# Accumulators regrouped by 256 rows in a six-layer cross network: PSUM layout, matmul width, head and tail order

## The chip, the cores and the metric

The kernel runs on one NeuronCore of a Trainium2 chip. The metric is the device time of one launch in microseconds (us). Engine names as in the profile: PE is TensorE's matmuls and PEld its weight loads, DVE is VectorE, ACT is ScalarE, POOL is GpSimd, SP is the engine that here only issues transfers.

## What is computed

Six layers of a cross network over 4096 rows of 416 features, in bf16:

```python
B, F, D, L = 4096, 26, 16, 6      # Din = 416
def reference(x0, ws, bs):
    x = x0
    for l in range(ws.shape[0]):
        x = x0 * (x @ ws[l] + bs[l]) + x
    return x
```

Since every x is x0 times something, the kernel keeps the running sum of all products, P = sum of x_l @ W_l, in PSUM, adds the summed bias c_l to it, and forms x = x0 * (P + c_l), where c_l holds the biases up to layer l and one. So the accumulators of a slab live in PSUM through all six layers.

## The kernel before

**Tiling.** Work is transposed: features lie on the partitions, rows on the free axis. The 4096 rows form four slabs s of SB = 1024; a slab has two halves of H = 512 rows and four groups g of G = 256. The 416 features are three chunks c (or m for outputs, k for inputs) of 128, and a tail of 32. The tail of a slab is packed: the 32 features of group g stand on the partitions 32g to 32g+31, so that `x0t_sb`, `xt_sb` and `t32_sb` are 128x256.

**PSUM.** Eight banks of 512 fp32 columns: bank `3*half + m` holds chunk m of one half, bank 6 (TAIL) the packed tail, bank 7 (SPARE) the transposes of input tails, biases and warm-up fills.

**One layer on TensorE** (program order, n = 6s + l):

1. *half A*, `main(0, wait_a)` (helper `tile_mm`, L174): 36 matmuls, 128 inputs to 32 outputs, 512 columns. Each four are the column tiles q = 0 to 3 of one chunk. `wait_a(k)` waits on s_xa for chunk k of the layer before.
2. *rows* (L272): twelve matmuls of 32 inputs (the tail features of group g) to 128 outputs, 256 columns, as row tiles. Two groups of one half share a bank; so they come in batches of 4, 2, 4 and 2, and batches 3 and 4 wait for s_row. Ahead of them are the waits on s_xt (the tail of x) and s_xb (half b). The last one increments s_ti.
3. *tail*: twelve column-tile matmuls of 256 columns into TAIL, and four with the corner weights `wc_sb`; s_to.
4. *half B*, `main(1, None)`: 36 matmuls as in half A, with s_mb after each chunk.

In slab 0 the transposes of the input tails of the next slabs (`tail_transposes`, eight small matmuls) follow half B of layers 1, 2 and 3; the first waits for s_xtl.

**The other engines.** DVE does six SCALAR_TENSOR_TENSOR a layer (L348): three for half a after s_ti, three for half b after s_mb, each reads a bank of 512 and gives x (s_xa, s_xb). ACT adds the tail's bias (`t32_sb`, L387, after s_to), POOL multiplies by x0 (`xt_sb`, L158, s_xt).

**Head.** SP issues in this order: xin (two loads of 256 rows), xtl of slab 0, the transposing load of x0T for rows 512 to 1023, w of layer 1, four loads of wt, w of layers 2 to 5, xtl of the other slabs (L100), x0T of the other slabs. ACT issues w of layer 0, the biases, and wt of layer 0 (four). TensorE meanwhile runs 20 fills, transposes xin (L198), makes the summed biases, and after half A of layer 0 transposes the tails of slab 0. ACT copies them to `x0t_sb` (L377), on which the rows of layer 0 wait (s_te).

**Tail.** For slabs 0 to 2 SP sends the result through DMA transposes. For slab 3 TensorE transposes (L312, L319): first the blocks of half a, then of half b once all of s_xb is there; ACT makes three copies of 128x768 and one of the tail, DVE one, and SP issues four output transfers (L125).

The order on each engine is the program's own[...] and each engine waits on its semaphores where they stand.

Of the kernel before, what the change touches and what calls it, by code (L numbers as in the profile page):

```python
# [6 lines left out]
FP32 = mybir.dt.float32  # L7
ALU = mybir.AluOpType
ACTF = mybir.ActivationFunctionType


def bass_standalone__dcn_v2_cross__recsys_kernel(
# [18 lines left out]
    TAIL, SPARE = 6, 7  # L31
    NFILL = 20

    with ExitStack() as es:
# [14 lines left out]
        t32_sb = sb("t32_sb", [128, 2, G], FP32)  # L49
        xo_sb = sb("xo_sb", [128, NS, NC, SB])  # L50
# [4 lines left out]
        ones_sb = sb("ones_sb", [128, 128])  # L55
# [18 lines left out]
        s_row, s_ti, s_to, s_mb = sem("s_row"), sem("s_ti"), sem("s_to"), sem("s_mb")  # L74
        s_xa, s_xb = sem("s_xa"), sem("s_xb")
        s_ta, s_xt = sem("s_ta"), sem("s_xt")
        s_oT, s_ot, s_otc = sem("s_oT"), sem("s_ot"), sem("s_otc")
        s_pT, s_out = sem("s_pT"), sem("s_out")
# [7 lines left out]

        @block.sync
        def _(sp):
            for h in range(2):
                sp.dma_start(xin_sb[:, 2 * h:2 * h + 2, :], x0_v[:, 2 * h:2 * h + 2, :]).then_inc(s_xin[h], 16)  # L90
            sp.dma_start(xtl_sb[:, 4:JS, :], x0_v[:, 4:JS, DF:D]).then_inc(s_xtl0, 16)
            sp.dma_start_transpose(x0T_sb[:, :, H:SB], x0[H:SB, 0:DF]).then_inc(s_x0T[0], 16)
# [27 lines left out]
            for i in range(4):  # L120
                j = (NS - 1) * JS + 2 * i
                if i == 0:
                    sp.wait_ge(s_oet, 1)
                sp.wait_ge(s_oe[i], 1)
                sp.dma_start(out_v[:, j:j + 2, :], o_sb[:, j:j + 2, :]).then_inc(s_out, 16)  # L125
# [3 lines left out]
        def _(pool):  # L129
            pool.memset(ones_sb[:, :], 1.0).then_inc(s_ones, 1)  # L130
            pool.memset(bsa_sb[0:1, :], 1.0).then_inc(s_set, 1)
            pool.wait_ge(s_ones, 1)
            pool.affine_select(
                out=ident[:, :], in_=ones_sb[:, :], pattern=[[-1, 128]],
                compare_op=ALU.is_equal, fill=0.0, base=0, channel_multiplier=1,
            ).then_inc(s_set, 1)
            pool.affine_select(
# [14 lines left out]
            for s in range(NS):  # L152
                pool.wait_ge(s_te, s + 1)
                for l in range(L):
                    n = s * L + l + 1
                    pool.wait_ge(s_ta, n)
# [15 lines left out]
        def _(pe):  # L172
            def tile_mm(dst, lhsT, rhs, q, start, stop):
                return pe.matmul(  # L174
                    dst, lhsT=lhsT, rhs=rhs, start=start, stop=stop,
# [3 lines left out]
            def tail_transposes(s):  # L179
                for r in range(2):  # L180
                    for g in range(4):
                        j = 2 * g + r
                        src = xin_sb[:, j, DF:D] if s == 0 and j < 4 else xtl_sb[:, s * JS + j, :]
                        ins = tile_mm(
                            ps[32 * g:32 * g + 32, SPARE, r * 128:(r + 1) * 128],
                            src, ident[:, :], g, True, True,
                        )
# [3 lines left out]
            for i in range(NFILL):  # L191
# [243 lines left out]
```

## Time and profile before

| | us |
|---|---|
| median of 13 runs | 141.57 |
| range of the runs | 140.57 to 142.50 |
| the profiled execution, its own time | 140.92 |
| its span, first to last instruction | 138.44 |
| PE busy | 130.8 (94%) |
| PEld busy | 68.3 (49%) |
| DVE busy | 98.7 (71%) |
| ACT, POOL busy | 17.8, 21.2 |
| one layer in the steady part | 5.13 |

The span leaves out what lies around the first and last instruction, here 2.5 us. Matmuls overlap, and their ends are modelled, so TensorE's work is read from the starts: the distance between the starts of two groups is what a group costs. A line such as L174 is that of a helper and gathers matmuls of several kinds.

### The profile page before, as it was taken

What the parts mean: (1) busy time and instruction counts of PE and PEld (TensorE: products, weight loads), DVE (VectorE), ACT (ScalarE), POOL (GpSimd) and SP (SyncE); (2) the same over time, 40 slices, a digit from 0 to 9 for tenths busy, and PEclk for the clock granted to TensorE, in tenths of its full rate; (3) what the DMA queues carried; (4) which work ended last, traced back from release to release, by engine and by line L of the source; (5) the groups of instructions that cost most, each with busy time, mean ns of one, the idle gap of its engine ahead of it and who ended that gap; (6) DMA issues with size and microseconds to landing.
All of it is one profiled execution on the core that took longest, in us unless ns stands there. A gap on an engine that the chain in (4) does not pass through costs nothing.

```text
span 138.4 us, 5386 instructions
## 1 busy us (share of the span) xinstructions
PE 130.8 (94%) x2506; PEld 68.3 (49%) x2506; DVE 98.7 (71%) x149; ACT 17.8 (13%) x36; POOL 21.2 (15%) x44
## 2 busy tenths in 40 slices
PE   6789999999999999999999999999999999999950
PEld 5435447645545445545545445545445545454440
DVE  0308778687688688679679679669669669669660
ACT  0611112111101101101101101101101101101170
POOL 5024111011011021011001111101101201101100
PEclk9999999999999999999999999999999999999999
DMA  4999799920009907000009651000009860000007
GB/s 105 283 252 335 88 231 219 171 60 0 5 0 92 166 1 250 0 0 5 5 0 119 132 195 56 5 0 5 5 0 193 58 231 20 5 0 7 0 2 245
DMA packets 32946, 12.26 MB, mean 89 GB/s; under 512 B 25239, under 2 KB 32925, under 8 KB 32925
## 3 DMA queue, kind: packets, MB, share of 16 engines
q1 hardware_dynamic: 32320, 11.50, 40.7%
q10 hardware_dynamic: 604, 0.43, 1.0%
q8 instruction: 19, 0.31, 0.9%
q14 instruction: 3, 0.02, 0.0%
HBM read 3.22 MB, written 3.41 MB: 48 GB/s over the span
## 4 chain that ended last, share of the span: by engine, by line
PE 90%; DVE 3%; DMA 3%; ACT 1%; SPq 0%; issue 0%
PE ps L174 77%; PE ps L272 12%; DVE xo_sb L348 3%; DMA xin_sb<-in_x_dram 3%; PE ps L312 1%; PE ps L198 1%; ACT o_sb L403 1%; SPq L90 0%; ACT x0t_sb L377 0%
## 5 line engine op out<-in xcount | busy, mean ns | idle before, releaser
L348 DVE SCALAR_TENSOR_TENSOR xT_sb<-ps,cb_sb,x0T_sb 128x512 bf16<-128x512 f32 x120 | 80.9, 743 | 25.6 <-PE ps L272 25.6
L174 PE MATMUL ps<-xT_sb,w_sb 128*32 128x512 bf16 (+1 forms) x1680 | 91.3, 364 | 0.0
L174 PEld LDWEIGHTS ps<-xT_sb,w_sb 128*32 128x32 bf16 x1680 | 44.0, 97 | 36.5 <-issue 0.5
L158 POOL TENSOR_TENSOR xt_sb<-t_sb,x0t_sb 128x256 bf16<-128x256 f32 x20 | 13.5, 674 | 84.6 <-ACT t_sb L387 84.6
L387 ACT ACTIVATE t_sb<-ps,cb_sb 128x256 f32<-128x256 f32 x24 | 11.4, 474 | 103.0 <-PE ps L174 103.0
L174 PE MATMUL ps<-x0T_sb,w_sb 128*32 128x512 bf16 (+1 forms) x336 | 19.7, 378 | 0.0
L348 DVE SCALAR_TENSOR_TENSOR xo_sb<-ps,cb_sb,x0T_sb 128x512 bf16<-128x512 f32 x24 | 16.2, 743 | 4.3 <-PE ps L272 4.3
L272 PE MATMUL ps<-xt_sb,wt_sb 32*128 32x256 bf16 x240 | 15.2, 275 | 0.0
L174 PEld LDWEIGHTS ps<-x0T_sb,w_sb 128*32 128x32 bf16 x336 | 8.8, 99 | 8.0 <-issue 1.0
L272 PEld LDWEIGHTS ps<-xt_sb,wt_sb 32*128 32x128 bf16 x240 | 6.0, 91 | 13.4 <-issue 8.5
L174 PE MATMUL ps<-xt_sb,wc_sb 128*32 128x256 bf16 x80 | 5.7, 273 | 0.0
L158 POOL TENSOR_TENSOR xot_sb<-t_sb,x0t_sb 128x256 bf16<-128x256 f32 x4 | 2.7, 675 | 17.8 <-ACT t_sb L387 17.8
L330 DVE COPY x0T_sb<-ps 128x256 bf16<-128x256 bf16 x4 | 1.2, 292 | 5.2 <-PE ps L198 4.9
L272 PE MATMUL ps<-x0t_sb,wt_sb 32*128 32x256 bf16 x48 | 3.0, 274 | 0.6 <-ACT x0t_sb L377 0.6
L192 PE MATMUL ps<-ones_sb 128*128 128x128 bf16 x20 | 2.3, 313 | 1.1 <-POOL ones_sb L130 1.1
L148 POOL COPY wc_sb<-wt_sb 32x32 bf16<-32x32 bf16 (+1 forms) x8 | 2.1, 258 | 5.4 <-DMA wt_sb<-in_ws_dram 4.9
L272 PEld LDWEIGHTS ps<-x0t_sb,wt_sb 32*128 32x128 bf16 x48 | 1.2, 91 | 3.0 <-issue 2.0
L198 PE MATMUL ps<-ident,xin_sb 128*128 128x128 bf16 x12 | 1.6, 307 | 1.0 <-DMA xin_sb<-in_x_dram 1.0
L403 ACT ACTIVATE o_sb<-ps 128x768 bf16<-128x768 bf16 x3 | 2.3, 809 | 2.2 <-PE ps L312 2.2
L192 PEld LDWEIGHTS ps<-ones_sb 128*128 128x128 bf16 x20 | 2.1, 147 | 1.1 <-POOL ones_sb L130 1.1
L377 ACT ACTIVATE x0t_sb<-ps 128x256 bf16<-128x256 f32 x4 | 1.5, 384 | 7.9 <-PE ps L174 7.9
L312 PE MATMUL ps<-ident,xo_sb 128*128 128x128 bf16 x24 | 1.7, 220 | 0.8 <-DVE xo_sb L348 0.8
(28 smaller groups left out, 16.4 us busy)
## 6 DMA issues: line engine op xcount, KB each, us to landing
out_dram<-o_sb SPq DMA_DIRECT2D x3, 832.0 KB, 4.1
w_sb<-in_ws_dram SPq DMA_DIRECT2D x5, 312.0 KB, 5.1
out_dram<-o_sb SPq DMA_DIRECT2D x4, 208.0 KB, 2.4
wt_sb<-in_ws_dram SPq DMA_DIRECT2D x4, 130.0 KB, 3.9
xin_sb<-in_x_dram SPq DMA_DIRECT2D x2, 208.0 KB, 3.5
w_sb<-in_ws_dram ACTq DMA_DIRECT2D x1, 312.0 KB, 3.7
xtl_sb<-in_x_dram SPq DMA_DIRECT2D x1, 192.0 KB, 7.2
o_sb<-xo_sb SPq DMA_TRANSPOSE x9, 4.4
```

The lines of the kernel that those rows point to most:

```text
L148: pool.tensor_copy(out=wc_sb[p, a:b, p], in_=wt_sb[p, a:b, DF:D]).then_inc(s_wc, 1)
L158: pool.tensor_tensor(out=dst, in0=t32_sb[:, n % 2, :], in1=x0t_sb[:, s, :], op=ALU.mult).then_inc(s_xt, 1)
L174: return pe.matmul(dst, lhsT=lhsT, rhs=rhs, start=start, stop=stop, skip_group_check=True, tile_position=(0, 32 * q),)
L192: pe.matmul(ps[:, SPARE, 0:128], lhsT=ones_sb[:, :], rhs=ones_sb[:, :], start=True, stop=True)
L198: ins = pe.transpose(out=psT[:, NC * (1 - h) + c, (j % 2) * 128:(j % 2 + 1) * 128], in_=xin_sb[:, j, c * 128:(c + 1) * 128], identity=iden ...
L272: ins = pe.matmul(ps[:, NC * (g // 2) + m, (g % 2) * G:(g % 2) * G + G], lhsT=wt_sb[p, l, m * 128:(m + 1) * 128], rhs=srct[p, :], start=l ...
L312: ins = pe.transpose(out=psT[:, banks[i], jj * DF + c * 128:jj * DF + (c + 1) * 128], in_=xo_sb[:, s, c, j * 128:(j + 1) * 128], identity= ...
L330: dve.tensor_copy(out=x0T_sb[:, c, h * 256:(h + 1) * 256], in_=psT[:, NC * (1 - h) + c, 0:256]).then_inc(s_inD, 1)
L348: dve.scalar_tensor_tensor(out=dst, in0=ps[:, NC * half + c, :], scalar=cb_sb[:, c, l:l + 1], in1=x0T_sb[:, c, o:o + H], op0=ALU.add, op1= ...
L377: act.activation(out=x0t_sb[:, s, :], in_=ps[:, SPARE, 0:G], func=ACTF.Copy).then_inc(s_te, 1)
L387: act.activation(out=t32_sb[:, n % 2, :], in_=ps[:, TAIL, 0:G], func=ACTF.Identity, bias=cb_sb[:, NC, l:l + 1],).then_inc(s_ta, 1)
L403: act.activation(out=o_sb[:, j0 + 2 * i:j0 + 2 * i + 2, 0:DF], in_=psT[:, (SPARE, 0, 3, 4)[i], 0:2 * DF].rearrange("p (j d) -> p j d", d=D ...
```

## The change

**PSUM layout.** `acc(m, g)` gives bank and first column: chunks 0 and 1 of group g share bank g, chunk 2 of group g has the first half of bank 4 + g. So group g, and with it row tile g, only ever writes the banks g and 4 + g. TAIL and SPARE move to the second halves of the banks 7 and 6. DVE reads a half of a chunk as two pieces of 256 out of two banks (`acc_half`, `split`).

**Matmul width.** Halves A and B are now done chunk by chunk (`chunk`), for each k with two groups of 256 columns in place of one of 512: 72 matmuls and weight loads a half in place of 36.

**Rows.** Three rounds of four with no s_row.

**Waits.** s_mb is raised twice a layer, after chunks 1 and 2, since chunks 0 and 1 share banks. Before chunk 2 of half B TensorE waits for s_ta (the bias activation has read TAIL). s_xa is awaited for two chunks at once.

**Input tails.** `tail_transposes` of slab s + 1 stand in layer 1 of slab s, between the tail and half B; the first of them still waits for s_xtl. Those of slab 0 go ahead of half A of layer 0.

**Head.** SP issues xin (first half), w of layer 0, xtl of slab 0, two of the four loads of wt of layer 0, then the transposing load; ACT issues xin (second half), the biases and the other two of wt. The fills are 13 of 256 columns, and three more between the two halves of xin's transposes.

**Tail.** In the last layer ACT adds the bias to chunk 2 of half a (into `a32_sb`) and POOL multiplies (s_a32, s_xaP), so DVE leaves it out. The last transposes are split: chunks 0 and 1 of half b before chunk 2. The last output transfer is issued by ACT.

```diff
+        def acc(m, g):
+            return (g, m * G) if m < 2 else (4 + g, 0)
+        def acc_half(m, half):
+            b, c = acc(m, 2 * half)
+            return ps[:, b:b + 2, c:c + G]
+        IN_BANKS = ((2, 3, 6), (4, 5, 2))
+        TAIL = ps[:, 7, G:2 * G]
+        SPARE = ps[:, 6, G:2 * G]
...
         def _(sp):
-            for h in range(2):
-                sp.dma_start(xin_sb[:, 2 * h:2 * h + 2, :], x0_v[:, 2 * h:2 * h + 2, :]).then_inc(s_xin[h], 16)
+            sp.dma_start(xin_sb[:, 0:2, :], x0_v[:, 0:2, :]).then_inc(s_xin[0], 16)
+            sp.dma_start(w_sb[:, 0, :, :], wmain(0)).then_inc(s_w[0], 16)
             sp.dma_start(xtl_sb[:, 4:JS, :], x0_v[:, 4:JS, DF:D]).then_inc(s_xtl0, 16)
+            for g in range(2):
+                sp.dma_start(wt_sb[32 * g:32 * g + 32, 0, :], ws[0, DF:D, :]).then_inc(s_wt[0], 16)
             sp.dma_start_transpose(x0T_sb[:, :, H:SB], x0[H:SB, 0:DF]).then_inc(s_x0T[0], 16)
...
+                    if n == NL:
+                        pool.wait_ge(s_a32, 1)
+                        pool.tensor_tensor(
+                            out=xo_sb[:, s, 2, 0:H], in0=a32_sb[:, :], in1=x0T_sb[:, 2, s * SB:s * SB + H], op=ALU.mult
+                        ).then_inc(s_xaP, 1)
...
             pe.wait_ge(s_ones, 1)
-            for i in range(NFILL):
-                pe.matmul(ps[:, SPARE, 0:128], lhsT=ones_sb[:, :], rhs=ones_sb[:, :], start=True, stop=True)
+            fill(13)
...
+            pe.wait_ge(s_xtl0, 16)
+            pe.wait_ge(s_inD, 2)
+            tail_transposes(0, 6, True)
...
-                    def main(half, waits):
...
+                    def chunk(m, half, before=None):
+                        for k in range(NC):
+                            if before:
+                                before(m, k)
...
+                            if COLUMN_TILES:
+                                for g in range(2 * half, 2 * half + 2):
+                                    b, c = acc(m, g)
+                                    for q in range(4):
+                                        f0 = m * 128 + 32 * q
+                                        ins = tile_mm(
+                                            ps[32 * q:32 * q + 32, b, c:c + G], w_sb[:, l, k, f0:f0 + 32],
+                                            src[:, k, off + g * G:off + (g + 1) * G], q,
+                                            l == 0 and k == 0 and m != 1 and half == 0,
+                                        )
+                        return ins
...
-                    for i, jobs in enumerate((
-                        ((0, 0), (1, 1), (2, 0), (3, 1)), ((0, 2), (2, 2)),
-                        ((0, 1), (1, 0), (2, 1), (3, 0)), ((1, 2), (3, 2)),
-                    )):
-                        if i >= 2:
-                            pe.wait_ge(s_row, 3 * n + i - 1)
-                        for g, m in jobs:
+                    for i in range(NC):
+                        for g in range(4):
+                            m = (i, (i + 2) % NC)[g // 2]
                             p = slice(32 * g, 32 * g + 32)
+                            b, c = acc(m, g)
                             ins = pe.matmul(
-                                ps[:, NC * (g // 2) + m, (g % 2) * G:(g % 2) * G + G],
+                                ps[:, b, c:c + G],
                                 lhsT=wt_sb[p, l, m * 128:(m + 1) * 128], rhs=srct[p, :],
...
-                        if i < 3:
-                            ins.then_inc(s_row, 1)
                     ins.then_inc(s_ti, 1)
...
-                    main(1, None)
-                    if s == 0 and 1 <= l <= NS - 1:
-                        if l == 1:
+                    if l == 1 and s < NS - 1:
+                        if s == 0:
                             pe.wait_ge(s_xtl, 16)
-                        pe.wait_ge(s_te, l)
-                        tail_transposes(l)
+                        tail_transposes(s + 1, 6, False)
+
+                    def before_b(m, k):
+                        if m == 2 and k == 0:
+                            pe.wait_ge(s_ta, n + 1)
+                            if l == 1 and s < NS - 1:
+                                pe.wait_ge(s_te, s + 2)
+
+                    chunk(0, 1, before_b)
+                    chunk(1, 1, before_b).then_inc(s_mb, 1)
+                    chunk(2, 1, before_b).then_inc(s_mb, 1)
...
                             dve.scalar_tensor_tensor(
-                                out=dst, in0=ps[:, NC * half + c, :], scalar=cb_sb[:, c, l:l + 1],
-                                in1=x0T_sb[:, c, o:o + H], op0=ALU.add, op1=ALU.mult,
+                                out=split(dst), in0=acc_half(c, half), scalar=cb_sb[:, c, l:l + 1],
+                                in1=split(x0T_sb[:, c, o:o + H]), op0=ALU.add, op1=ALU.mult,
                             ).then_inc((s_xa, s_xb)[half], 1)
...
         def _(act):
-            act.dma_start(w_sb[:, 0, :, :], wmain(0)).then_inc(s_w[0], 16)
+            act.dma_start(xin_sb[:, 2:4, :], x0_v[:, 2:4, :]).then_inc(s_xin[1], 16)
             act.dma_start(bsa_sb[1:L + 1, :], bs[:, :]).then_inc(s_bs, 16)
-            for g in range(4):
+            for g in range(2, 4):
                 act.dma_start(wt_sb[32 * g:32 * g + 32, 0, :], ws[0, DF:D, :]).then_inc(s_wt[0], 16)
...
+                    if n == NL:
+                        act.wait_ge(s_ti, n)
+                        act.activation(
+                            out=split(a32_sb[:, :]), in_=acc_half(2, 0), func=ACTF.Identity, bias=cb_sb[:, 2, l:l + 1],
+                        ).then_inc(s_a32, 1)
...
+            act.wait_ge(s_oe[3], 2)
+            act.wait_ge(s_oet, 1)
+            act.dma_start(out_v[:, j0 + 6:j0 + 8, :], o_sb[:, j0 + 6:j0 + 8, :]).then_inc(s_out, 16)
```

## Prediction

> **What bounds the kernel now.** First the page: which engine carries the chain that ended last, and who waits for whom.
>
> ```profile
> span 138.4 us, 5386 instructions
> ...
> PE 90%; DVE 3%; DMA 3%; ACT 1%; SPq 0%; issue 0%
> PE ps L174 77%; PE ps L272 12%; DVE xo_sb L348 3%; DMA xin_sb<-in_x_dram 3%; PE ps L312 1%; PE ps L198 1%; ACT o_sb L403 1%; SPq L90 0%; ACT x0t_sb L377 0%
> ...
> L348 DVE SCALAR_TENSOR_TENSOR xT_sb<-ps,cb_sb,x0T_sb 128x512 bf16<-128x512 f32 x120 | 80.9, 743 | 25.6 <-PE ps L272 25.6
> ```
>
> TensorE holds 90% of the chain; DVE waits for it (25.6 us), not the reverse. Then the timeline of one steady layer (start, us, engine, count), to split TensorE's 5.13 us:
>
> ```profile
> 72.79 0.51 PE L174 MATMUL ps<-x0T_sb,w_sb 128*32 128x256 bf16 x12
> ...
> 73.23 2.12 PE L174 MATMUL ps<-x0T_sb,w_sb 128*32 128x512 bf16 x36
> ...
> 75.18 2.12 PE L174 MATMUL ps<-xT_sb,w_sb 128*32 128x512 bf16 x36
> ...
> 77.22 0.76 PE L272 MATMUL ps<-xt_sb,wt_sb 32*128 32x256 bf16 x12
> ...
> 77.92 0.51 PE L174 MATMUL ps<-xT_sb,w_sb 128*32 128x256 bf16 x12
> ...
> 78.25 0.28 PE L174 MATMUL ps<-xt_sb,wc_sb 128*32 128x256 bf16 x4
> ...
> 78.36 0.39 PE L174 MATMUL ps<-xT_sb,w_sb 128*32 128x512 bf16 x4
> ```
>
> Ends of matmuls overlap, so only starts are read. Four column tiles run side by side. Half B (73.23 to 75.18) is 9 groups of four: 0.216 us each. Half A to the rows (75.18 to 77.22) is the same plus 0.095 for the change to row tiles. The twelve row matmuls of L272 take 0.70 (77.22 to 77.92) where three groups at 0.11 would be 0.33. Narrow windows show why: the 2nd, 3rd and 4th batches start at
>
> ```profile
> 77.34 0.27 PE L272 MATMUL ps<-xt_sb,wt_sb 32*128 32x256 bf16 x2
> 77.59 0.29 PE L272 MATMUL ps<-xt_sb,wt_sb 32*128 32x256 bf16 x4
> 77.71 0.28 PE L272 MATMUL ps<-xt_sb,wt_sb 32*128 32x256 bf16 x2
> ```
>
> so batch 2 costs 0.12 for two matmuls, and the s_row wait 0.24 before batch 3. Last, the head: when the load lands that the change puts in front of layer 1's half B.
>
> ```profile
> L100 SPq DMA_DIRECT2D xtl_sb<-in_x_dram x1: 542/542/542, 9.7 to 9.7; - x1
> ...
> DMA to landing us min/median/max: 7.2/7.2/7.2
> ```
>
> Issued at 9.71, xtl lands at 16.9. Today it is needed at 18.3 (TensorE's transposes after B of layer 1): no wait.
>
> [...] groups at 6.58, 7.00, 7.43, 7.86 (0.43), then 0.216 from about 8.2. [...] the windows from 3 to 15 us show a DMA share of 1.05 to 1.43, saturated. [...]
>
> **Part by part, against the profiled run (span 138.4, its own time 140.92, so 2.5 around the span).**
>
> *Row tiles, removed cost.* Three rounds of four, each row tile in banks of its own, no s_row: 0.11 + 0.11 + 0.20 (the last round to the tail, as 77.71 to 77.92) = 0.43 against 0.70: **-0.27 per layer**.
>
> *256 columns in place of 512, added.* 72 matmuls become 144, with 72 more weight loads. Nearest row: the tail groups of 128x256, whose starts are 110, 109 and 109 ns apart (77.92 to 78.25 is three groups). 36 groups x 109.2 = 3.93 against 18 x 215.8 = 3.885: **+0.047 per layer**. The loads (97 ns each, four beside each other) fit in 109 by 12 ns; that cover is thin.
>
> Net -0.22, a period of 4.91. Of 24 layers, 22 (from B of layer 1 to B of layer 23) count: -4.8.
>
> *Does DVE then bound?* L348 starts at 0.31 after the last row batch; five pitches of 0.66 and 0.743 end at 4.36; the xb wait to the first row matmul takes at least 0.11 (9.855 to 9.96 in layer 0), the rows 0.22: 4.7 against 4.91. Reading two banks with a split pattern is not in the trace; from zero to 10 ns each (ACT's four-dimensional L397 takes 392 against 383): 4.76, still hidden. The new s_mb rule lets DVE's b0 start only after chunk 1, since chunks 0 and 1 share banks: chunk 1 is visible 2.15 after the last row batch, DVE is free at 2.30. Hidden by 0.15. s_ta ahead of chunk 2: ACT's 0.47 ends about 0.6 us before it is needed.
>
> *Head.* xin's second half and half of wt move to ACT, w0 and the rest to SP ahead of the x0T transpose, so that five issues (0.5 each) precede it in place of three: w1 and all behind it, xtl too, are issued about 1.0 later (10.7). DMA is saturated, so much of that is backlog; but while SP spends 2.7 us issuing the transpose (3.3 to 6.0) little else is queued, and I estimate that xtl lands 0.3 to 1.0 later, **17.5** taken (16.9 to 18.2 kept). TensorE's own head gains: 16 fills of 256 replace 20 of 128, the first tail transposes move ahead of A, and ACT's x0t copy (0.38, from 9.43) and the idle around it leave the path: rows of layer 0 at about 8.4 to 9.3 in place of 9.96. POOL's larger memset (0.2 before) and its new order end before xin lands at 3.9; its wc copies get wt no later than now (7.3). w1, 1.0 later, lands near 10; A of layer 1 asks for it near 12. Layer 1 then reaches its tail's end at about 14.8 to 15.3 in place of 16.3.
>
> *Where that gain goes.* The transposes of slab 1 now stand before B of layer 1, behind s_xtl. TensorE, arriving near 15, stops until 17.5: **2.2 to 2.7 us idle**, with everything on its queue behind it. After the landing, 0.1 for the wait and 0.11 for eight transposes: B starts at 17.7 against 16.36 before: **+1.35**. The head's gain is worth nothing; it only lengthens the wait. A second effect: [...] after, the landing sets the pace. So the sum stands for the median too, though the profiled 140.92 is 0.65 under the median of 141.57.
>
> *Transposes and a hiccup inside the 22 periods.* Before, B of layer 1 to B of layer 23 took 113.29 = 22 x 5.128 + 0.47; after, two transpose blocks, 0.22: -0.25.
>
> *Tail.* Before, from the start of the last B (129.65) to the end 8.73, with
>
> ```profile
> 129.31 4.04 DVE L348 SCALAR_TENSOR_TENSOR xo_sb<-ps,cb_sb,x0T_sb 128x512 bf16<-128x512 f32 x6 [1.09 <-PE ps L272]
> ...
> 134.06 1.98 SPq L125 DMA_DIRECT2D out_dram<-o_sb  x4
> ```
>
> four output issues of 0.5 in a row on SP, the last at +5.88, landing 2.5 later. After, ACT and POOL take chunk 2 of half a. ACT's 128x512 is not in the trace: between 0.47 and 0.95, 0.69 taken; POOL's between 0.67 and 1.35, 1.2 taken; both end before B's last matmul (+1.86). POOL's product stands ahead of its xot product (0.68), which then ends near +2.4; TensorE asks for it at +2.7. ACT's five copies (0.81, 0.81, 0.39, about 0.60 between its neighbours, 0.39) run from +2.6 to about +5.2, then ACT issues; SP's third goes at about +5.4. Last landing 7.9 in place of 8.4: **-0.5** (0 to -0.8).
>
> Sum: -4.8 + 1.35 - 0.25 - 0.5 = -4.2; 140.9 - 4.2 = **136.7**. Bounds: xtl -0.6/+0.7, layers 1.3 either way (60 ns each), tail -0.3/+0.5; about 135 to 138.5.
>
> **Rivals.**
> *No stop at xtl* (8%). If xtl landed by 15, B of layer 1 would start near 15.2: 2.5 less, about 134.2. Against: 3.5 MB lies ahead of xtl in a queue that is saturated until 15.
> *The 256-column groups can't be fed* (14%), the case on the slower side. In steady state TensorE must take eight instructions per 109 ns, 13.6 each. [...] The turning point is low: 4.2 us over 864 groups is 5 ns, so past a pitch of 114 ns the change loses. Instruction blocks arrive through DMA too: 19 blocks of 16 KB now, some 13 more then, each in 0.9 to 1.5 us; a stall of 0.35 on each would also cancel it. Against: after a wait that blocks TensorE's sequencer until 9.91, 128 instructions were handed over by 11.63, at most 13.5 ns each[...]. That is just enough, and it is an upper bound. Three pitches at 109 in every layer show that the array can; 18 in a row are not shown.
> *A partial loss* (9%): DVE over 68 ns slower per L348 (0.41 us over six, from 4.7 to 5.13) makes DVE the bound and takes all of the layers' gain; or an idle stretch of over 2 us lets the clock fall[...]. The first needs a split pattern to cost 10%[...].
>
> **How the numbers follow.** Forecast 69%, 136.7 (135 to 138.5). With the 8% below and the clock's case above, 134.2 to 139.4 leaves out about 2 in 10. Faster by over 0.3% (0.4 us, about what a measurement of this kernel can tell): 69 + 8 + about 6 of the 9 = 0.83; same 0.02; slower 14 + 1 = 0.15.
>
> **What would show it.** Right: row matmuls in three rounds of four with starts 0.11 apart; 256-column groups at 109 ns; layers at 4.91; a wait of 2 us or more before the transposes of slab 1, ended by xtl at 17 to 18; no such wait for slabs 2 and 3. Wrong: TensorE "issue" idle or pitches over 114 in mid-layer; DVE without idle time; xtl landed before TensorE comes.

## The result: slower, 147.1 us in place of 141.3

The kernel after takes 147.08 us (median of 11 runs, 145.11 to 149.87) against 141.26 for the kernel before on the same chips: ratio 1.039, 95% interval 1.034 to 1.045. The prediction was 136.7 and a range of 134.2 to 139.4. The profiled execution takes 148.07 and its span is 146.35. Medians here and below are over all executions; ratios leave out those more than 1.5% above the kernel's fastest, and with them the profiled one of kernel after (the others have a median of 146.59).

The page of the profile, kernel after. The queue lines give blocks, MB and share; the chain gives shares of the span:

```profile
span 146.3 us, 8843 instructions
...
q8 instruction: 33, 0.54, 1.5%
...
PE 79%; SPq 6%; issue 5%; DMA 5%; ACT 1%
...
L414 DVE SCALAR_TENSOR_TENSOR xT_sb<-ps,cb_sb,x0T_sb 128x512 bf16<-128x512 f32 x120 | 81.5, 744 | 32.3 <-PE ps L312 27.6
```

DVE is as fast as before (744 ns against 743) and waits for TensorE even longer. New in the chain is 5% of "issue": time in which TensorE waited for nothing that the profile shows. The queue q8, which carries the instructions, brought 33 blocks of 16 KB (19 before). The view of waits, TensorE only (line, releaser: us in all, times, longest):

```profile
PE ps L198 <- issue: 5.1, 9, 1.5
PE ps L198 <- DMA xtl_sb<-in_x_dram: 2.1, 2, 1.9
PE ps L312 <- issue: 1.6, 2, 1.0
```

The stop at s_xtl is the predicted one. The waits at L198 for "issue" are not in it. The timeline shows where they stand (start, us, engine, line and operation, count, and idle before in brackets). First a layer of slab 2:

```profile
70.95 0.51 PE L312 MATMUL ps<-xt_sb,wt_sb 32*128 32x256 bf16 x12
71.39 0.51 PE L198 MATMUL ps<-xT_sb,w_sb 128*32 128x256 bf16 x12
71.72 0.28 PE L198 MATMUL ps<-xt_sb,wc_sb 128*32 128x256 bf16 x4
71.83 2.13 PE L198 MATMUL ps<-xT_sb,w_sb 128*32 128x256 bf16 x71
74.18 0.28 PE L198 MATMUL ps<-xT_sb,w_sb 128*32 128x256 bf16 x1 [0.22 <-issue]
74.31 2.15 PE L198 MATMUL ps<-x0T_sb,w_sb 128*32 128x256 bf16 x72
76.39 0.51 PE L312 MATMUL ps<-x0t_sb,wt_sb 32*128 32x256 bf16 x12
```

Rows to tail is 0.44, as predicted (0.43). Half A, 74.31 to the rows at 76.39, is 18 groups at 109 ns and the change of tiles. So the array can take 18 groups in a row, and with them eight instructions in each 109 ns. But one matmul before the end of half B TensorE stops, in the middle of a group of four, where no semaphore stands. It is the same in slab 3, and worse:

```profile
120.55 1.47 PE L198 MATMUL ps<-xT_sb,w_sb 128*32 128x256 bf16 x45
123.54 2.91 PE L198 MATMUL ps<-xT_sb,w_sb 128*32 128x256 bf16 x99 [1.51 <-issue]
```

Counted through the trace, such stops come before matmul 474, 601, 729, 856, 983, 1238, 1365 and so on: 127 or 128 apart, or a multiple of it. With its weight load a matmul is two instructions, so that is 254 to 256 instructions; and the page has 8460 of TensorE's in 33 blocks of 16 KB, 256 to a block.

The records of the blocks themselves, which lie in the same trace, say what TensorE waits for. At each of 19 block ends of kernel after there is a stop of 0.2 to 1.8 us from one start to the next, and each time the first matmul of the new block starts 1.2 to 1.6 us after the end of that block's own transfer. The transfers take 0.9 to 1.4 us, under long stops and short ones alike. What differs is when they begin, counted from the first matmul of the block before: 1.0 to 1.75 us at the stops up to 0.6 us, and 2.1 to 3.3 us at the five longer ones. Each of these five follows other transfers, input loads or the results of a slab, in the 2 us before it.

How much this costs is read from layers. Where nothing stalls, the rows of two layers are 4.920 apart (predicted 4.91). From the start of half B of layer 1 (18.16) to that of layer 23 (137.14) are 118.98 us. Take off 22 x 4.920 and 0.22 for two blocks of transposes: **10.5 us of stalls**. That is 0.35 for each of the 30 blocks fetched in that time. (It is the sum of this one execution; the median of the kernel is 1.0 us lower.)

### The profile page after: what moved, and what is told of

It reads as the page before. It is cut to its first block, busy times and chain, and to the rows that moved or that the text cites. A ratio compares the mean times of both kernels' runs of the same rounds, so it can differ in the third digit from the quotient of the medians.

```text
span 146.3 us, 8843 instructions
## 1 busy us (share of the span) xinstructions
PE 130.8 (89%) x4230; PEld 111.6 (76%) x4230; DVE 98.9 (68%) x149; ACT 18.2 (12%) x38; POOL 22.4 (15%) x45
## 4 chain that ended last, share of the span: by engine, by line
PE 79%; SPq 6%; issue 5%; DMA 5%; ACT 1%
PE ps L198 72%; PE ps L312 7%; DMA xtl_sb<-in_x_dram 5%; SPq L113 2%; SPq L116 1%; SPq L111 1%; SPq L110 1%; ACT o_sb L464 1%; PE ps L350 1%; SPq L108 0%; ACT o_sb L476 0%; SPq L106 0%; SPq L107 0%; ACT o_sb L469 0%
## 5 line engine op out<-in xcount | busy, mean ns | idle before, releaser
L198 PE MATMUL ps<-xT_sb,w_sb 128*32 128x256 bf16 x3120 | 95.7, 273 | 4.7 <-issue 4.5
L198 PEld LDWEIGHTS ps<-xT_sb,w_sb 128*32 128x32 bf16 x3120 | 81.8, 97 | 13.9 <-issue 12.2
L198 PE MATMUL ps<-x0T_sb,w_sb 128*32 128x256 bf16 x624 | 19.9, 273 | 0.3 <-issue 0.2
L198 PEld LDWEIGHTS ps<-x0T_sb,w_sb 128*32 128x32 bf16 x624 | 16.5, 97 | 2.1 <-issue 1.9
L312 PE MATMUL ps<-xt_sb,wt_sb 32*128 32x256 bf16 x240 | 10.4, 271 | 1.6 <-issue 1.6
L312 PEld LDWEIGHTS ps<-xt_sb,wt_sb 32*128 32x128 bf16 x240 | 4.6, 92 | 6.1 <-issue 5.9
L198 PE MATMUL ps<-xt_sb,wc_sb 128*32 128x256 bf16 x80 | 5.6, 273 | 0.0
L205 PE MATMUL ps<-ones_sb 128*128 128x256 bf16 x16 | 3.8, 419 | 1.2 <-POOL ones_sb L149 1.2
L198 PE MATMUL ps<-ident,xtl_sb 128*32 128x128 bf16 x28 | 1.4, 222 | 2.4 <-DMA xtl_sb<-in_x_dram 1.9
L198 PEld LDWEIGHTS ps<-ident,xtl_sb 128*32 128x32 bf16 x28 | 0.7, 95 | 2.9 <-DMA xtl_sb<-in_x_dram 2.1
L198 PEld LDWEIGHTS ps<-xt_sb,wc_sb 128*32 128x32 bf16 x80 | 2.1, 97 | 0.0
L312 PE MATMUL ps<-x0t_sb,wt_sb 32*128 32x256 bf16 x48 | 2.0, 271 | 0.0
```

The costliest lines, as they stand in the source:

```text
L198: return pe.matmul(dst, lhsT=lhsT, rhs=rhs, start=start, stop=True, skip_group_check=True, tile_position=(0, 32 * q),)
L205: pe.matmul(ps[:, 7, 0:256], lhsT=ones_sb[:, 0:128], rhs=ones_sb[:, :], start=True, stop=True)
L312: ins = pe.matmul(ps[:, b, c:c + G], lhsT=wt_sb[p, l, m * 128:(m + 1) * 128], rhs=srct[p, :], start=l == 0 and g >= 2 and i < 2, stop=True ...
```

## The experiments

**Theory 1:** instruction blocks come too late. Each four column tiles of 256 columns are eight instructions in 109 ns, so that a block of 256 is used up in about 127.5 x 4.92 / 172 = 3.65 us (172 matmuls a layer; 127.5 for stops 127 or 128 apart), in place of 127.5 x 5.128 / 100 = 6.5 before. The 4 us that the expectations have for a fetch is an estimate; 3.65 and the 0.35 of stall a block come to that. **Rivals:** the column tiles or their weight loads stall by themselves; the new layout and its waits hold somebody up; the stop at s_xtl and the new head are the loss.

| run | TensorE instructions a layer | blocks | median us | ratio to before |
|---|---|---|---|---|
| after | 344 | 33 | 147.08 | 1.039 |
| e1_wide | 128 | 13 | 141.10 | 0.998 (0.993 to 1.003) |
| e2_pad | 128 | 13 | 141.20 | 0.998 (0.995 to 1.001) |
| e3_bsplit (layout of before) | 344 | 33 | 147.93 | none; before 141.24 |
| e4_t64 | 200 | 19 | 141.64 | 0.994 (0.991 to 0.998) |
| e5_late | 344 | 33 | 145.89 | 1.028 (1.018 to 1.038) |
| e6_wide_late | 128 | 13 | 136.69 | 0.966 (0.959 to 0.973) |
| e9_noout | 344 | 33 | 143.12 | 1.011 (1.008 to 1.014) |
| e10_mixed | 272 | 26 | 140.78 | 1.002 (0.998 to 1.005) |
| e11_bwide (layout of before) | 92 | 9 | 144.39 | 1.016 (1.010 to 1.023) |
| e12_fill | 128 | 13 | 140.21 | 0.988 (0.982 to 0.994) |
| e13_quiet | 209 on average | 20 | 136.91 | 0.966 (0.960 to 0.971) |
| e14_busy | 209 on average | 20 | 140.02 | 0.987 (0.979 to 0.996) |
| e15_oet | 128 | 13 | 136.54 | 0.962 (0.956 to 0.968) |
| e16_head | 128 | 13 | 135.79 | 0.959 (0.953 to 0.964) |

**Fewer instructions, the same array work (e1_wide).**

```diff
-COLUMN_TILES = True
+COLUMN_TILES = False
```

> Kernel after, with each group of four 32-column matmuls of the halves A and B made one matmul of 128 columns: the same PSUM layout, widths of 256, waits, head and tail, but 128 TensorE instructions (weight loads and matmuls) a layer in place of 344. Theory 1, instruction blocks come too late (16 KB each, 256 instructions, used up in 3.64 us where one fetch takes 4): a block now lasts 9.8 us, so the idle stretches put down to issue (8.5 us in the sum) go; 147.1 - 8.5 = 138.6, up to 141 if the change between full array and column tiles costs 0.1 a layer. Rival, the new layout or its waits hold DVE or TensorE up (split reads of two banks, s_mb after two chunks, s_ta): nothing of that changes, 147. Rival, the stop at s_xtl and the new head make the loss: 147, with TensorE stopped near 18 us as before.

Measured: 141.10. No "issue" stop is left in the layers; every layer from 23.7 us on takes 5.025 (5.138 with transposes in it). So theory 1 holds against the layout and its waits. But the time stands at the upper end of what was expected, and the view of windows (us, busy time of each engine, then granted clock, DMA share, GB/s) shows why:

```profile
14.70:17.70 3.00, 0.20 (x8) 0.00 (x0) 1.78 (x3) 0.47 (x1) 0.67 (x1) 1.00 0.65 65
18.20:21.40 3.20, 3.20 (x18) 2.20 (x17) 0.86 (x2) 0.29 (x1) 0.00 (x0) 0.51 1.12 233
22.00:25.00 3.00, 3.00 (x48) 2.19 (x46) 1.36 (x3) 0.20 (x1) 0.00 (x0) 1.00 1.15 236
```

TensorE comes to s_xtl at about 14.7, more than a microsecond before kernel after does, and stands still until 17.7. Then the clock is 0.51 for 3.2 us, and fifteen groups come at 213 ns in place of 109: 1.6 us. With the stop of 3.0 that is most of what had been won back. It did not happen each time: four of the twelve executions of e1_wide took 139.5 to 139.8 us at a mean clock of 0.99, the other eight 141.0 to 141.7 at 0.98.

**No-operations as padding (e2_pad).**

```diff
+                                        for _ in range(6):
+                                            pe.nop(nofuse=True)
```

> e1_wide with six no-operations after each matmul of the halves, so that TensorE again gets 344 instructions a layer, while the array does the work of e1_wide. Theory 1 (the supply of instructions): the stalls come back, one at each 256 instructions, 0.1 to 1.7 us; 146 to 149 if a no-operation takes no more than the 13.6 ns that eight instructions in 109 ns leave; if it takes 20 ns, the pitch is 147 ns, a block lasts 4.7 us, no stalls but 24 x 36 x 38 ns = 33 us more. Rival, weight loads of column tiles do it (they are gone here): like e1_wide, 138 to 141.

A miss. The page counts 3659 instructions and 13 blocks, exactly as in e1_wide: the no-operations never reached the program. The run is a repetition of e1_wide (141.20) and tells nothing between the theories.

**More instructions in the old layout (e3_bsplit).**

```diff
-                                for q in range(4):
+                                for e in range(2):
+                                    for q in range(4):
...
-                                        w_sb[:, l, k, f0:f0 + 32], src[:, k, o:o + H], q,
+                                            w_sb[:, l, k, f0:f0 + 32], src[:, k, o + e * G:o + (e + 1) * G], q,
```

> Kernel before, its layout, rows with s_row, head and tail untouched, only with each 512-column matmul of the halves cut into two of 256 in the same bank: 344 TensorE instructions a layer in place of 200. Theory 1: a block lasts 127.5 pairs x (5.18 / 172) = 3.84 us, below the 4 of a fetch, so stalls of 0.1 to 1.5 us at each 256 instructions, +3 to +8: 144 to 149. Rival, the layout, the waits or the head of the change make the loss: only the pitch counts, 36 x 109.2 against 18 x 215.8 ns, +0.047 a layer, +1.1: 142.4.

Measured: 147.93 (145.43 to 149.01), 6.7 over before; the shortest execution, the one profiled, is 4.2 over it and longer than every execution of before measured beside it (139.77 to 142.63). Nothing of the new layout, waits, head or tail is in this kernel, so what its layers lose belongs to the cut into 256 columns. The span of the profiled execution is 5.0 longer than that of before. Of this, 1.3 is the head: the groups of half A of layer 0 come at half rate until 10.2 us there (until 8.2 in before); this is no stop at a block's end. The layers add 3.7. Without a stall they take 5.172, 0.044 more than before, as the pitches say, 1.0 in all; the other 2.7 are stops in mid-group, here behind 65 of 72 matmuls of a half:

```profile
56.21 2.02 PE L174 MATMUL ps<-xT_sb,w_sb 128*32 128x256 bf16 x65
58.59 0.62 PE L174 MATMUL ps<-xT_sb,w_sb 128*32 128x256 bf16 x16 [0.36 <-issue]
```

**Column tiles of 64 (e4_t64).**

```diff
-                                    for q in range(4):
-                                        f0 = m * 128 + 32 * q
+                                    for q in range(2):
+                                        f0 = m * 128 + 64 * q
```

> Kernel after with column tiles of 64 in place of 32: 200 instructions a layer, as before the change. Theory 1: a block lasts 127.5 x 4.91 / 100 = 6.3 us, longer than a fetch, no stalls: 138.6. Rival, column tiles as such (side by side, weight loads in the shadow of other tiles) are at fault: some stalls stay, 141 to 147. Rival, layout and waits: 147.

Measured: 141.64. Tiles side by side, and as many instructions as before the change: no stall. The time is that of e1_wide and for the same reason (a stop of 3.4 us at s_xtl, then a granted clock of 0.57 from 18.2 to 21.4 us; here too a part of the executions, 139.5 to 141.0, had a mean clock of 0.99).

**No stop at s_xtl (e5_late, e6_wide_late).** In PE, and likewise in ACT:

```diff
-                    if l == 1 and s < NS - 1:
+                    if l == (2 if s == 0 else 1) and s < NS - 1:
                         if s == 0:
                             pe.wait_ge(s_xtl, 16)
```

> Kernel after (column tiles of 32), only with the transposes of slab 1's input tails in layer 2 of slab 0 in place of layer 1, so that TensorE does not stop for s_xtl. Theory 1 (instruction blocks come too late): the stop of 2.1 us goes, the idle put down to issue (8.5 us) stays, 147.1 - 2.0 = 145. Rival, the stop at s_xtl and what it entails are the whole loss: 147.1 - 5.8 or more, below 141.3.

Measured: 145.89. Taking the stop away brought 1.2 us by the medians, and the stalls stayed, as the view of waits shows; so the stop isn't the loss. In this trace too there are stops at 19 block ends, and each ends 1.2 to 1.6 us after its block's transfer.

```profile
PE ps L198 <- issue: 4.5, 7, 1.5
```

> e1_wide (one matmul of 128 columns in place of four of 32) with the transposes of slab 1's tails in layer 2. In e1_wide TensorE stood still from 14.63 to 17.76 us, and then the pitch was 213 ns in place of 109 for fourteen groups. Theory: the clock fell because of the stop; both go: 141.1 - 3.0 - 14 x 0.104 = 136.6. Rival, something else sets the end of e1_wide (DVE, the granted clock, the tail): 139 to 141. Rival, the stop goes but the slow groups stay, whatever comes before them: 138.

Measured: 136.69, **5.3 us faster than before**. Without the stop the slow groups after it are gone too. With the stalls and the stop gone, the gain of the rest of the change is there. That the time is also the predicted 136.7 is chance: the prediction had 1.35 for the stop, which is gone here, and nothing for what follows. One thing costs more than in kernel after. A layer of e6_wide_late, timeline:

```profile
97.75 2.13 PE L263 MATMUL ps<-x0T_sb,w_sb 128*128 128x256 bf16 x18
99.81 0.51 PE L312 MATMUL ps<-x0t_sb,wt_sb 32*128 32x256 bf16 x12
100.24 0.51 PE L198 MATMUL ps<-x0T_sb,w_sb 128*32 128x256 bf16 x12
100.58 0.28 PE L198 MATMUL ps<-x0t_sb,wc_sb 128*32 128x256 bf16 x4
100.80 2.14 PE L263 MATMUL ps<-x0T_sb,w_sb 128*128 128x256 bf16 x18
```

From the corner group (100.58) to half B are 0.22, where kernel after needs 0.11 (71.72 to 71.83): going from column tiles to the full array is one more change of tile shape a layer, 5.025 in place of 4.920.

**Waits as padding (e7_sem236, e8_sem344).** Three and six more instructions after each matmul of the halves (two waits go into one instruction; q8 brings 23 and 33 blocks). The edit of e7_sem236 is shown; e8_sem344 has 12 waits in place of 6:

```diff
+                                        for _ in range(6):
+                                            pe.wait_ge(s_set, 4)
```

> e6_wide_late with three more instructions after each of the 864 matmuls of the halves: waits on a semaphore that has long had its value. 236 TensorE instructions a layer, a block of 256 lasts 5.3 us, longer than a fetch of 4. Theory 1: no stalls, like e6_wide_late, 136.6, as long as five instructions go into 109 ns. Rival (every instruction beyond one a matmul costs its own time): above 138, with a pitch over 109 ns in every group.

> e6_wide_late with six such waits after each matmul: 344 TensorE instructions a layer, as many as kernel after, with the matmuls of e6_wide_late. A block of 256 lasts 3.64 us. Theory 1: the stalls come back, each at a multiple of 256 instructions, 0.1 to 1.7 us, 8 us in the sum: 143 to 146. Rival, the weight loads of 32-column tiles or their banks do it: like e6_wide_late, 136.6. If a wait takes more than 13.6 ns, each group's pitch rises instead (20 ns each: 147 ns, 33 us).

Measured: 341.37 and 621.86 us. A miss as a test of the supply: a wait that is fulfilled long since costs far more than a slot. The pitch of a matmul is 338 ns in e7_sem236, and in e8_sem344

```profile
101.23 0.37 PE L263 MATMUL ps<-xT_sb,w_sb 128*128 128x256 bf16 x1 [0.28 <-issue]
101.89 0.37 PE L263 MATMUL ps<-xT_sb,w_sb 128*128 128x256 bf16 x1 [0.29 <-issue]
```

655 to 690: three more instructions cost 317 ns or more, **106 ns each** at the least, and 106 ns is also the distance at which the waits themselves start in both traces.

**What makes a block late (e9_noout, e13_quiet, e14_busy).** In e5_late stalls crowd where slab outputs are on the DMA queues. From e5_late the stores, output transposes and tail copies of slabs 0 to 2 are taken out:

```diff
-            for s in range(NS - 1):
-                n = (s + 1) * L
...
-            sp.wait_ge(s_out, 16 * (NS + 3))
+            sp.wait_ge(s_out, 16 * 4)
```

> e5_late with the results of slabs 0, 1 and 2 never sent out (no output transposes, no copies of their tails, no stores); all the rest as there. In e5_late the stalls at block ends after 40 us sum to 3.8 us, nearly all of them within 5 us of these transfers. Theory 1a, a fetch is late where other transfers share the DMA engines with it: they go, 145.9 - 3.5 = 142.4; those before 32 us, under the input loads, stay. Theory 1b, a fetch takes longer than a block lasts by itself: they stay, 145 to 146.

Measured: 143.12, 2.8 less than e5_late. Over the eighteen layers after about 40 us the excess over 4.920 (transposes taken off) is 2.0 us against 4.9 in e5_late: the transfers make three fifths of these stalls, and the rest stays without them. So 3.65 us a block is just about what a fetch takes by itself: the legs read in kernel after, at their usual 1.1 us to the transfer, 1.1 for it and 1.4 from its end to the first matmul, make about 3.6. The next two kernels look at it from the other side. In both, nine layers of e6_wide_late get column tiles of 32 again, once in the layers 3 to 5 of slabs 1 to 3 (e13_quiet, shown), once in the layers 0 to 2 (e14_busy):

```diff
-COLUMN_TILES = True
+TILED = (9, 10, 11, 15, 16, 17, 21, 22, 23)
...
+                    COLUMN_TILES = n in TILED
```

> e6_wide_late with column tiles of 32 again in nine of the 24 layers, layers 3 to 5 of slabs 1 to 3, when no output of a slab is on its way: 344 TensorE instructions in these layers, 128 in the others. Theory 1a (a block is late where transfers share the DMA engines): nearly no stalls, and nine layers of 4.92 in place of 5.025: 136.7 - 0.95 = 135.8. Theory 1b (a block lasts too short by itself): 0.2 to 0.3 us of stall at each of some 13 blocks in these layers: 138 to 139.

> As e13_quiet, with the nine tiled layers put at layers 0 to 2 of slabs 1 to 3, when the output of the slab before is transposed and stored. The same number of instructions. Theory 1a: the stalls that e5_late has in these stretches (3.3 us in the sum) come back, in part or whole: 137.8 to 139. Theory 1b: as e13_quiet, whichever its time is. No effect of instructions at all: 135.8.

Measured: 136.91 and 140.02. The same instructions, 3.1 us apart; the two profiled executions are 2.2 apart, and in that of e14_busy the stops in its tiled layers sum to 2.3. The timeline of a tiled layer of e13_quiet:

```profile
95.44 0.51 PE L314 MATMUL ps<-xt_sb,wt_sb 32*128 32x256 bf16 x12
95.87 0.51 PE L198 MATMUL ps<-xT_sb,w_sb 128*32 128x256 bf16 x12
96.21 0.28 PE L198 MATMUL ps<-xt_sb,wc_sb 128*32 128x256 bf16 x4
96.32 2.14 PE L198 MATMUL ps<-xT_sb,w_sb 128*32 128x256 bf16 x72
98.39 1.81 PE L265 MATMUL ps<-x0T_sb,w_sb 128*128 128x256 bf16 x15
```

and of e14_busy:

```profile
76.78 1.58 PE L198 MATMUL ps<-xT_sb,w_sb 128*32 128x256 bf16 x49
78.87 2.80 PE L198 MATMUL ps<-xT_sb,w_sb 128*32 128x256 bf16 x95 [0.51 <-issue]
```

In the quiet stretches 72 matmuls come in a row, and the second and third tiled layers take 4.919. Under the output they break off after 49, at a block's end. The quiet stretches are only three layers long; e9_noout, which is tiled throughout and has no other transfers from about 40 us to its tail, has layers of 4.92 there and others with stops of up to 0.45 us. e13_quiet didn't reach its 135.8: at the join with wide layers one more change of shape costs 0.11, so three tiled layers gain 0.1 in place of 0.3, and its profile has the rows of layer 1 1.1 us late (see e16_head).

**Half the dose (e10_mixed).**

```diff
+                                    T = (32, 64)[half]
+                                    for q in range(128 // T):
+                                        f0 = m * 128 + T * q
```

> e5_late with half A in column tiles of 32 and half B in column tiles of 64: 272 TensorE instructions a layer between the 128 of e6_wide_late and the 344 of e5_late. Theory 1: a block lasts 256 / 272 x 5.03 = 4.7 us, more than a fetch of 4; nearly no stalls, a layer of 5.03 (the change from 32 to 64 columns costs the 0.105 that e6_wide_late shows), 137 to 138. Rival, tiles of 32 columns are slow by themselves: half the stalls of e5_late stay, 140 to 141.

Measured: 140.78, 3 us above the expectation, but not from stalls: after 20 us there are none. Every layer takes 5.155. There are two more changes of shape, from 32 to 64 columns and back to 32, each about 0.12: 4.920 + 0.235. The expectation had counted one. So 4.85 us a block (256 / 272 x 5.155) is slow enough even under the transfers. And half A of this kernel has column tiles of 32 at the full pitch, 72 matmuls in a row (the first line, the rows follow), so these tiles and their weight loads do not stall by themselves:

```profile
69.85 2.15 PE L275 MATMUL ps<-x0T_sb,w_sb 128*32 128x256 bf16 x72
71.93 0.51 PE L314 MATMUL ps<-x0t_sb,wt_sb 32*128 32x256 bf16 x12
```

**The wide matmul alone (e11_bwide).**

```diff
-                                for q in range(4):
-                                    f0 = m * 128 + 32 * q
...
+                                ins = pe.matmul(
+                                    ps[:, NC * half + m, :], lhsT=w_sb[:, l, k, m * 128:(m + 1) * 128],
```

> Kernel before, only with each group of four 32-column matmuls of 512 in the halves made one of 128 columns (92 TensorE instructions a layer in place of 200). Theory 1: before had no stalls to lose; the change from column tiles to the full array costs 0.105 a layer as in e6_wide_late (5.025 against 4.920): 141.5 + 2.5 = 144. Rival, matmuls of 128 columns are what makes e6_wide_late fast, not the layout and head of the change: below 140.

Measured: 144.39; layers of 5.233, that is 5.128 + 0.105. So e6_wide_late does not owe its gain to the full array, which costs; it owes it to the rest of the change.

**The clock after the stop (e12_fill).**

```diff
                         if s == 0:
+                            pe.wait_ge(s_z, 1)
+                            for _ in range(26):
+                                pe.matmul(
+                                    ps[:, 2, 0:G], lhsT=zero_sb[:, :], rhs=ones_sb[:, :],
...
                             pe.wait_ge(s_xtl, 16)
```

> e1_wide with 26 matmuls of zeros put ahead of the wait for s_xtl (2.8 us of work that adds nothing), so that TensorE stops for 0.3 us in place of 3.1. Theory, the idle stretch makes the clock fall: the fourteen groups at 213 ns after it go back to 109, 141.1 - 1.5 = 139.6. Rival, what slows them comes from elsewhere (the landing transfers, the weights): 141.

Measured: 140.21, 0.9 below e1_wide. From 18.2 to 21.4 us the granted clock is 1.00 and the groups are 109 ns apart (view of windows as above):

```profile
18.20:21.40 3.20, 3.20 (x37) 2.78 (x34) 1.55 (x3) 0.38 (x1) 0.00 (x0) 1.00 1.17 241
```

The wait for s_xtl and the landing transfers are there as before. TensorE stands idle for 0.2 us there, against 3.0 and a clock of 0.51 after it in e1_wide. So it is the idle array that brings the clock down.

**The tail (e15_oet).** TensorE's transposes of the output tail go between its first and second six, and ACT's copy of them likewise:

```diff
                 ).then_inc(s_oe[i], 2)
-            act.wait_ge(s_pt, 1)
-            act.activation(
+                if i == 0:
+                    act.wait_ge(s_pt, 1)
+                    act.activation(
```

> e6_wide_late with the copy of the output tails (s_oet) on ACT ahead of its second copy of 128x768 in place of after it, and the two transposes that it reads ahead of the second six on TensorE: SP's first store of the last slab can go at 130.0 in place of 130.6, while the last issue stays where it is. Before and e6_wide_late both end 4.37 us after the first of these stores, though the last issue stood 0.57 nearer to the rows in e6_wide_late. Theory (the stores fill the DMA engines, 0.83 MB, so the first sets the end): -0.6, 136.1. Rival (the end is the last issue and 2.5, as predicted): 136.7.

Measured: 136.54 against 136.69, which by itself is too little to tell. The profile tells it: from the rows of the last layer to the end are 9.46 us in place of 10.07. ACT and SP, timeline:

```profile
130.20 0.38 ACT L471 ACTIVATE o_sb<-ps 128x256 bf16<-128x256 bf16 x1
130.46 0.82 ACT L465 ACTIVATE o_sb<-ps 128x768 bf16<-128x768 bf16 x1
130.60 1.62 SPq L144 DMA_DIRECT2D out_dram<-o_sb  x3
131.15 0.90 ACT L478 ACTIVATE o_sb<-ps 128x512 bf16<-128x512 bf16 x2
132.08 0.41 ACTq L481 DMA_DIRECT2D out_dram<-o_sb  x1
```

The first store goes 5.00 after the rows (5.70 in e6_wide_late), the next two 0.41 and 0.34 earlier than there, the last one 0.15 (6.48 against 6.63, SP's third), and the end moves by 0.61. So the last issue does not set the end. It stays 4.4 to 4.5 behind the first store, but as the second and third moved too, the first alone isn't shown to set it.

**The rows of layer 1 (e16_head).**

```diff
-                        pe.wait_ge(s_wc, 4 * (l + 1))
...
+                    if s == 0 and l < 2:
+                        pe.wait_ge(s_wc, 4 * (l + 1))
                     for g in range(4):
                         p = slice(32 * g, 32 * g + 32)
                         ins = tile_mm(TAIL[p, :], wc_sb[:, l, p], srct, g, False)
```

The transposes of slab 1's tails go to layer 3 as well; in the trace of e15_oet nothing waits at them in layer 2.

> e15_oet with TensorE's wait for the corner weights (s_wc) moved from the rows to the four matmuls that read them, in the layers 0 and 1 of slab 0, and the transposes of slab 1's tails in layer 3. In kernel after, e6_wide_late and e15_oet the rows of layer 1 start 0.1 after POOL's four corner copies (1.43 us, begun when wt of layers 1 to 5 landed) end, at 14.0 to 15.1, where half A would let them start at 13.9. Theory (these copies hold the rows): the rows of layer 1 start near 13.9, the corner matmuls wait for at most 0.3 of it instead, and TensorE no longer waits for s_xtl: -0.3 to -0.9 against e15_oet, 136.0. Rival (wt itself, or the block of instructions that falls there, holds them): no change, 136.5.

Measured: 135.79 (135.63 to 135.89), 0.75 below e15_oet, as expected, and the fastest version: **4.1% faster than before** (0.953 to 0.964). In the traces of kernel after, e6_wide_late and e15_oet the rows start 0.10 after the fourth of POOL's corner copies ends (15.02, 13.94, 14.60), and so they do in e10_mixed, e12_fill, e13_quiet and e14_busy; in e1_wide, where the copies end at 13.18, the rows don't wait. In e16_head they start 5.025 after those of layer 0, with no wait. Since the copies in that one profile ended at 13.51, ahead of half A's end, the profile doesn't show the gain. The medians speak for it, but they come from two chips, and the intervals of the two ratios overlap.

## Why the prediction was wrong

**The step that failed is "256 columns in place of 512".** Its term was +0.047 a layer for the pitch and nothing for the supply of instructions. The pitch was right (109 ns through 18 groups, layers of 4.920). The supply cost 10.5 us in the profiled execution. The sentence was there, "instruction blocks arrive through DMA too", with 0.35 on each of 13 more blocks as the point where the gain is gone. What was missing is a division that the page of before allowed: 5012 TensorE instructions in 19 blocks are 264 to a block, and at 13.6 ns they are used up in 3.6 us within a half (3.5 for the 256 of kernel after). Against that the prediction held the transfer alone, 0.9 to 1.5, and took it for the whole fetch. In kernel after the transfer begins 0.8 us or more after TensorE has entered the block before, and the first matmul follows 1.2 to 1.6 us behind its end. It is the rate of use, not the count of added blocks, that decides: 0.35 fell on all 30 blocks, not on 13. The evidence taken against that rival, 128 instructions handed over at 13.5 ns each, was no more than half a block and could not speak for the next one.

How the profiled execution's 148.07 comes out of the predicted 136.7: +10.74 for the 22 layers (10.5 stalls, and 4.92 for 4.91), +0.45 for the start of half B of layer 1 (18.16 against 17.7; xtl landed at 18.0, not 17.5), +0.92 for the tail (9.21 from the last half B, where 0.5 was to come off 8.79; the prediction's 8.73 is a slip, 129.65 to 138.44), and 1.72 around the span in place of 2.48 (-0.76). That makes 148.05.

**The stop at s_xtl** was right in its place and nearly in its size. The timeline of kernel after:

```profile
15.90 0.28 PE L198 MATMUL ps<-xt_sb,wc_sb 128*32 128x256 bf16 x4
18.04 0.29 PE L198 MATMUL ps<-ident,xtl_sb 128*32 128x128 bf16 x8 [1.85 <-DMA xtl_sb<-in_x_dram]
18.16 2.03 PE L198 MATMUL ps<-xT_sb,w_sb 128*32 128x256 bf16 x68
```

TensorE came 1 us later than predicted, since the rows of layer 1 waited for the corner copies: POOL's wait for wt of layers 1 to 5 had been priced for layer 0 only.

```profile
13.59 1.43 POOL L167 COPY wc_sb<-wt_sb 32x160 bf16<-32x160 bf16 x4 [2.36 <-DMA wt_sb<-in_ws_dram]
...
15.12 0.51 PE L312 MATMUL ps<-xt_sb,wt_sb 32*128 32x256 bf16 x12 [0.95 <-issue]
```

So the stop was about 2 us, and the clock stayed up (1.00 from 18.2 to 21.4 us).

**The clock** as a partial loss came true where it wasn't looked for: in e1_wide, e2_pad and e4_t64, which reach s_xtl a microsecond sooner: in their traces the corner copies end by 13.7 and no block is late, and the rows of layer 1 start at 13.85 to 13.89. What an idle stretch costs was the author's estimate in the prediction. Measured: in e1_wide a stop of 3.1 us cost fifteen groups at 213 ns in the profiled execution, and by the mean clocks in eight of twelve. A stop of 2 us, in kernel after, left the granted clock at 1.00. How long a stop has to be for the clock to fall is not shown.

**Row tiles** were right: three rounds, 0.44 in place of 0.70. (In the lines of before it is the first batch, of four, that takes 0.12, and the second 0.25 with the wait; the sum of 0.70 stands.) DVE was right: split reads cost 1 ns. **The tail** was wrong by its principle. ACT's 0.69 was met, POOL took 1.16 for 1.2, and in e6_wide_late the last issue did come nearer to the rows than before: by 0.39, SP's third at 6.63 against 7.02 (the 0.57 of the expectation for e15_oet takes ACT's store for the last). But the end did not follow the last issue. From that to the end of the span are 2.9 us in before and 3.4 in after and e6_wide_late. In all three it is the first store and 4.37 to 4.38 us, in which the 0.83 MB of four stores go out, and the first store waits for ACT's copy of the tail, which the change left where it was (5.72 after the rows, 5.55 before):

```profile
141.56 0.39 ACT L469 ACTIVATE o_sb<-ps 128x256 bf16<-128x256 bf16 x1
141.82 0.90 ACT L476 ACTIVATE o_sb<-ps 128x512 bf16<-128x512 bf16 x2
141.97 1.44 SPq L144 DMA_DIRECT2D out_dram<-o_sb  x3
```

What gets longer in a fetch beside other transfers is the time until the block's transfer begins, up to 3.3 us; the transfer takes 0.9 to 1.5 us either way. Why it begins late stays open, as the trace doesn't show when a block is asked for.

## What to carry to other kernels

Price a change of matmul size by instructions per time as well as by array time: 256 instructions used up in 3.65 us stalled, in 4.85 us they did not, and a stop in the middle of a group where no semaphore stands is the sign. Before cutting matmuls into column tiles ask what one full matmul costs, and count the changes of tile shape in a loop, about 0.11 us each. Where several stores end a kernel, look at when the first can start, and not only at the last.

## What the runs showed of the hardware

- A change of tile shape on TensorE costs 0.105 to 0.12 us, also between column tiles of 32 and of 64 (layers of 4.920, with one change more 5.025 in e6_wide_late and 5.040 in e4_t64, with two more 5.155 in e10_mixed).
- A wait instruction on TensorE that is fulfilled already costs about 106 ns when it stands between matmuls (e7_sem236, e8_sem344), and with three after every matmul the mean granted clock is 0.65.
- In kernel after TensorE goes from one block of instructions to the next no sooner than 1.2 us after the end of the next block's transfer where it had to wait for it, and this transfer begins 0.8 us or more after it has entered the block before. Used up in 3.65 us, a block leaves next to no room.
- Instructions come in blocks of 16 KB on the DMA queue q8 (33 in kernel after), and other transfers hold them up: 344 instructions a layer ran at full pitch in quiet stretches (4.919) and lost up to 0.8 us in a layer beside stores and DMA transposes (5.818 in e14_busy, 0.11 of it its tail transposes).
